# Eight pairs of heads get their mask from TensorE and their exponentials slot by slot on ScalarE; weight words travel on GpSimd's queue

## The chip, the cores and the metric

One core of one Trainium2 chip. The metric is the device time of one execution in microseconds; lower is better. Of the kernel before, three runs are known, and one further execution that was profiled.

## What is computed

Windowed attention over 8 batches and 8 heads (576 positions, 64 channels), plain windows of 32 in the first four heads and windows of 32 with a step of 4 in the other four, followed by a gated two-layer block with a convolution of three taps. Cut to what matters:

```python
scores = scale * (q @ k.T)
mask   = (rel >= 0) & (rel < 32)                  # heads 0 to 3
       | (rel >= 0) & (rel < 128) & (rel % 4 == 0)  # heads 4 to 7
scores = where(mask, scores, -1e9)
scores = scores - max(scores)
attn   = exp(scores); attn = attn / (sum(attn) + 1e-9)
x      = concat_heads(attn @ v)
h      = maximum(x @ w_in, 0)
c      = conv_w[0] * h[s-1] + conv_w[1] * h[s] + conv_w[2] * h[s+1]
out    = (h * sigmoid(c)) @ w_out
```

w_in, conv_w and w_out are given as 64-bit floats; q, k and v as 32-bit floats.

## The kernel before, in words

**Work.** A batch has four pairs of heads (`attention`, L228; pairs 0 and 1 plain, 2 and 3 with the step) and one `expert` (L352). A pair goes through these steps. *Scores* (L248): small matmuls into the PSUM buffer `att`, 18 blocks of 32 queries by 64 keys for each head, laid out as nine slots of 64 columns. *Softmax*: DVE adds the mask while it reads `att` (L254, L257), which frees `att`; it takes the maximum of each slot (L260) and subtracts it (L262); ScalarE takes the exponential of all nine slots in one instruction (L264); DVE sums (L266), adds 1e-9 (L268), takes the reciprocal (L270), multiplies (L271) and transposes into `pt` (L273). *Values* (L283): small matmuls from `pt` and `v` into `att` again. *Split*: x is kept as a high and a low part; ScalarE copies the high part out (L330), and the low part is what is left. For the first two batches (`HELPED = 2`) TensorE subtracts the high part inside `att` (`less`, L337 and L340) and ScalarE copies the rest (L343); from the third batch on DVE subtracts (L345).

There is one buffer `att` of four banks, so the scores of one pair and the values of another take turns in it; `pt` and `qk` have two buffers, `s`, `z`, `v` and `out` three.

The expert multiplies x with w_in, three matmuls of 288 columns per 128 by 128 block (high by high, high by low, low by high; L363), ScalarE applies the ReLU (L370), the convolution and the gate alternate between ScalarE and DVE (L381, L375 twice, L386, L388, L390, L392) and give the eight parts g0 to g7, and the second product takes those (L405), copied out by L412. Each product of a batch has 192 matmuls.

**Weights** (`weights`, L423). A block of 128 by 512 64-bit words is loaded into a buffer `out` (L431), and turned into a high and a low part: L438 on ScalarE, L440, L443, L445, L448, L451 on DVE. For the first ten blocks TensorE adds the pieces (L460, L461, L462) and ScalarE copies both parts (L457, L465); for the last six DVE does it (L467, L473).

**Order.** Nothing of this is in program order. `Planner.order` (L113) is a list scheduler with booked costs, latencies and due times; it runs when the kernel is built and writes each engine's instructions in the order of its plan. `DUE`, `PAIR`, `WI`, `WO`, `AHEAD` and `PERIOD` (L196 to L203) are those due times. On the chip each engine executes its own list in order, and what is late holds up what stands behind it. `SP` is one such list: loads of qk (L235) and v (L237), weight words (L431) and the outputs.

```python
last = plan.add("DVE", 0.68, due + 1.5, lambda: nc.vector.tensor_tensor(
    out=halves(flat()[:, 0:512]), in0=sc.t[:, 0:2, 0:256], in1=halves(mask_sb[:, kind, 0:512]), op=ALU.add),
```

Of the kernel before, what the change touches and what calls it, by code (L numbers as in the profile page):

```python
# [54 lines left out]
SCALE = 1.0 / D ** 0.5  # L55
# [18 lines left out]
class Planner:  # L74

    LATENCY = {"DVE": 0.05, "ACT": 0.05, "SP": 2.0, "E": 0.2, "S": 0.33, "T": 0.35, "V": 0.2}
    OVERLAP = {"DVE": 0.08, "ACT": 0.095}
# [80 lines left out]
def attn_moe(ctx: ExitStack, tc: tile.TileContext, qk_p, qk_d, v_p, v_d, w_in, w_out, conv, mask, out):  # L158
    nc = tc.nc
    const = ctx.enter_context(tc.tile_pool(name="const", bufs=1))  # L160
# [37 lines left out]
    WI, WO = (-20.4, -20.4, -7.2, -7.2, -3.1, -0.1, 7.8, 7.8), (17.2, 17.2, 36.3, 36.3, 36.9, 34.9, 43.2, 43.2)  # L198
    AHEAD = (9.1, 0.8, 0.7)
    PERIOD = 55.1  # L200
    for b in range(2, B):
        DUE[b] = tuple(t + PERIOD * b for t in (-5.1, 5.4, 33.0))
        PAIR[b] = tuple(t + PERIOD * b for t in (-21.7, -18.8, -17.2, -13.1))  # L203
    SUMMED = 10
    HELPED = 2

# [21 lines left out]
    def attention(b, p):  # L228
# [22 lines left out]
        last = plan.add("PE", (0.8, 0.92)[kind], due, scores, [lq], [qk, sc, s], "S")  # L251
        flat = lambda: s.t.rearrange("p a k -> p (a k)")
        halves = lambda t: t.rearrange("p (h k) -> p h k", h=2)
        last = plan.add("DVE", 0.68, due + 1.5, lambda: nc.vector.tensor_tensor(  # L254
            out=halves(flat()[:, 0:512]), in0=sc.t[:, 0:2, 0:256], in1=halves(mask_sb[:, kind, 0:512]), op=ALU.add),
            [last], [sc, s])
        last = plan.add("DVE", 0.215, due + 1.5, lambda: nc.vector.tensor_tensor(  # L257
            out=flat()[:, 512:576], in0=sc.t[:, 2, 0:W], in1=mask_sb[:, kind, 512:576], op=ALU.add), [last], [sc, s])
        wide = lambda t: t.unsqueeze(2).to_broadcast([128, 9, W])
        last = plan.add("DVE", 0.755, due + 2.0, lambda: nc.vector.tensor_reduce(  # L260
            out=m.t, in_=s.t, axis=AX.X, op=ALU.max), [last], [s, m])
        last = plan.add("DVE", 0.755, due + 2.5, lambda: nc.vector.tensor_tensor(  # L262
            out=s.t, in0=s.t, in1=wide(m.t), op=ALU.subtract), [last], [s, m])
        last = plan.add("ACT", 0.685, due + 3.0, lambda: nc.scalar.activation(  # L264
            out=s.t, in_=s.t, func=AF.Exp, scale=SCALE), [last], [s], "exp")
# [36 lines left out]

        last = plan.add("PE", (0.9, 0.85)[kind], due + 6.0, values, [lv, last], [v, pt, tv, x], "V")

# [23 lines left out]
        his = []  # L328
        for i, cost in ((1, (0.25, 0.3)[kind]), (0, (0.62, 1.12)[kind])):
            last = plan.add("ACT", cost, due + 7.0, lambda i=i: nc.scalar.copy(out=dst(x.t[0], i), in_=val(i)),  # L330
                            [last, *his], [tv, x])
            his.append(last)
        if b < HELPED:
            def less():
                main, rest = parts(x.t[0])
                for t in range(4):
                    nc.tensor.matmul(tv.t[:, t, 0:128], minus, main[:, t], start=False, stop=True,  # L337
                                     skip_group_check=True)
                for g in range(2):
# [83 lines left out]
    def weights(src, n, due, dst=None, pair=None, summed=False):  # L423
# [59 lines left out]
    nc.vector.tensor_copy(out=slot_masks[0][:, 0:5:4, :], in_=kinds_sb[:, 0:2, :])  # L483
    nc.vector.tensor_copy(out=slot_masks[1], in_=spread(2, 9))
    nc.vector.tensor_copy(out=slot_masks[1][:, 0:5:4, :], in_=spread(3, 2))
    nc.vector.tensor_copy(out=slot_masks[1][:, 8, :], in_=kinds_sb[:, 4, :])
    for h, in hs:
# [89 lines left out]
```

## Time and profile before

| | |
|---|---|
| median of three runs | 549.02 us (548.75 to 549.81) |
| the profiled execution | 548.65 us, of it 546.9 us span |
| PE busy | 520.8 us, 95% of the span |
| DVE busy | 410.0 us, 75% |
| ACT busy | 289.7 us, 53% |
| granted TensorE clock, mean of the span | 0.991 |

The span runs from the first to the last instruction that the profiler recorded; the profiled execution's own time is 1.75 us longer. A busy share is a mean over stages that differ, so it says little by itself: the rows further down are read by stretch.

### The profile page before, as it was taken

What the parts mean: (1) busy time and instruction counts of PE and PEld (TensorE: products, weight loads), DVE (VectorE), ACT (ScalarE), POOL (GpSimd) and SP (SyncE); (2) the same over time, 40 slices, a digit from 0 to 9 for tenths busy, and PEclk for the clock granted to TensorE, in tenths of its full rate; (3) what the DMA queues carried; (4) which work ended last, traced back from release to release, by engine and by line L of the source; (5) the groups of instructions that cost most, each with busy time, mean ns of one, the idle gap of its engine ahead of it and who ended that gap; (6) DMA issues with size and microseconds to landing.
All of it is one profiled execution on the core that took longest, in us unless ns stands there. A gap on an engine that the chain in (4) does not pass through costs nothing.

```text
span 546.9 us, 19084 instructions
## 1 busy us (share of the span) xinstructions
PE 520.8 (95%) x8664; PEld 496.5 (91%) x8664; DVE 410.0 (75%) x695; ACT 289.7 (53%) x556; POOL 0.9 (0%) x12
## 2 busy tenths in 40 slices
PE   3599978999999999999999999999999999999997
PEld 2578877999999999999999999999989999999997
DVE  5978999899996389937997399837987289936910
ACT  2466775755742586227742586227732486327721
POOL 0000000000000000000000000000000000000000
PEclk9999997999999999999999999999999999999999
DMA  7765614331135003530144103530045102300011
GB/s 251 267 196 177 207 42 155 100 121 44 50 99 162 18 23 109 163 104 23 52 146 150 30 23 96 170 111 23 28 146 168 35 23 65 112 26 23 0 44 45
DMA packets 17073, 52.32 MB, mean 96 GB/s; under 512 B 2016, under 2 KB 3168, under 8 KB 16992
## 3 DMA queue, kind: packets, MB, share of 16 engines
q1 hardware_dynamic: 16848, 51.02, 28.4%
q8 instruction: 68, 1.11, 0.9%
q10 hardware_dynamic: 144, 0.08, 0.1%
q14 instruction: 13, 0.11, 0.1%
HBM read 41.66 MB, written 9.44 MB: 93 GB/s over the span
## 4 chain that ended last, share of the span: by engine, by line
PE 88%; DVE 8%; ACT 2%; DMA 2%; issue 1%; DVEq 0%; ACTq 0%
PE nn L405 38%; PE mm L363 33%; PE att L283 8%; PE att L248 5%; DVE c L375 2%; PE nn L460 1%; DMA qk<-in_qk_d_dram 1%; PE att L337 1%; DVE s L254 1%; DVE s L262 1%; DVE c L388 1%; DVE m L260 1%; DMA qk<-in_qk_p_dram 1%; DVE pt L273 1%; DVE s L271 1%
## 5 line engine op out<-in xcount | busy, mean ns | idle before, releaser
L375 DVE SCALAR_TENSOR_TENSOR c<-h,conv_sb,c 128x576 f32<-128x576 f32 x128 | 104.0, 815 | 53.2 <-ACT c L381 51.6
L370 ACT ACTIVATE h<-mm 128x288 f32<-128x288 f32 x120 | 48.8, 408 | 49.7 <-PE mm L363 49.5
L412 ACT COPY out<-nn 128x288 f32<-128x288 f32 x64 | 25.3, 397 | 76.4 <-PE nn L405 70.9
L283 PEld LDWEIGHTS att<-pt,v 32*64 32x64 f32 x3072 | 41.4, 140 | 14.8 <-DVE s L257 4.6
L388 DVE TENSOR_TENSOR c<-c,h 128x576 f32<-128x576 f32 x64 | 47.6, 755 | 9.2 <-ACT c L386 7.7
L283 PE MATMUL att<-pt,v 32*64 32x64 f32 (+2 forms) x3072 | 44.9, 234 | 9.3 <-DVE s L257 3.5
L381 ACT ACTIVATE c<-h,conv_sb 128x576 f32<-128x576 f32 x64 | 49.6, 776 | 1.3
L248 PE MATMUL att<-qk 64*32 64x64 f32 x2432 | 36.2, 235 | 10.9 <-DMA qk<-in_qk_d_dram 5.6
L248 PEld LDWEIGHTS att<-qk 64*32 64x32 f32 x2432 | 30.1, 111 | 16.8 <-issue 5.7
L386 ACT ACTIVATE c<-c 128x576 f32<-128x576 f32 x64 | 42.5, 679 | 2.8 <-DVE c L375 2.3
L363 PE MATMUL mm<-x2a,wi 128*128 128x288 f32 x144 | 40.5, 296 | 0.0
L363 PE MATMUL mm<-x1a,wi 128*128 128x288 f32 x144 | 40.3, 296 | 0.0
L363 PE MATMUL mm<-x3a,wi 128*128 128x288 f32 x144 | 40.3, 295 | 0.0
L363 PE MATMUL mm<-x0a,wi 128*128 128x288 f32 x144 | 40.3, 295 | 0.0
L405 PE MATMUL nn<-g2a,wo 128*128 128x288 f32 x128 | 36.9, 303 | 0.0
L405 PE MATMUL nn<-g6a,wo 128*128 128x288 f32 x128 | 36.7, 300 | 0.0
L405 PE MATMUL nn<-g0a,wo 128*128 128x288 f32 x128 | 36.4, 299 | 0.2
L405 PE MATMUL nn<-g1a,wo 128*128 128x288 f32 x128 | 36.5, 300 | 0.0
L405 PE MATMUL nn<-g3a,wo 128*128 128x288 f32 x128 | 36.4, 299 | 0.0
L405 PE MATMUL nn<-g5a,wo 128*128 128x288 f32 x128 | 36.4, 299 | 0.0
L405 PE MATMUL nn<-g4a,wo 128*128 128x288 f32 x128 | 36.4, 299 | 0.0
L405 PE MATMUL nn<-g7a,wo 128*128 128x288 f32 x128 | 36.0, 300 | 0.1
(194 smaller groups left out, 1482.6 us busy)
## 6 DMA issues: line engine op xcount, KB each, us to landing
qk<-in_qk_d_dram SPq DMA_DIRECT2D x16, 664.0 KB, 4.4
qk<-in_qk_p_dram SPq DMA_DIRECT2D x16, 592.0 KB, 5.0
out_dram<-out SPq DMA_DIRECT2D x28, 288.0 KB, 2.3
v<-in_v_d_dram SPq DMA_DIRECT2D x16, 384.0 KB, 3.4
v<-in_v_p_dram SPq DMA_DIRECT2D x16, 384.0 KB, 3.5
out<-in_w_in_dram SPq DMA_DIRECT2D x8, 512.0 KB, 5.4
out<-in_w_out_dram SPq DMA_DIRECT2D x8, 512.0 KB, 4.6
out_dram<-out SPq DMA_DIRECT2D x8, 144.0 KB, 1.8
```

The costliest lines, as they stand in the source:

```text
L248: nc.tensor.matmul(sc.t[quad * 32:quad * 32 + 32, slot // 4, slot % 4 * W:slot % 4 * W + W], q, k, start=i == 0, stop=i == len(parts) - 1, ...
L254: last = plan.add("DVE", 0.68, due + 1.5, lambda: nc.vector.tensor_tensor(out=halves(flat()[:, 0:512]), in0=sc.t[:, 0:2, 0:256], in1=halve ...
L260: last = plan.add("DVE", 0.755, due + 2.0, lambda: nc.vector.tensor_reduce(out=m.t, in_=s.t, axis=AX.X, op=ALU.max), [last], [s, m])
L283: nc.tensor.matmul(tv.t[hd * 64:hd * 64 + 64, bank, o:o + n], v.t[quad * 32:quad * 32 + 32, block // 2, block % 2 * 64:block % 2 * 64 + 64 ...
L363: nc.tensor.matmul(ps.t[:, 0:HALF], wi[jw][fc][:, k * 128:k * 128 + 128], x[k].t[jx][:, hf * HALF:hf * HALF + HALF], start=(k == 0 and i = ...
L370: relu.append(plan.add("ACT", 0.4, due + 1.6 * u + 1.6, lambda fc=fc, hf=hf, ps=ps: nc.scalar.activation(out=h[fc].t[:, 1 + hf * HALF:1 + ...
L375: nc.vector.scalar_tensor_tensor(out=c[fc].t, in0=h[fc].t[:, k:S + k], scalar=conv_sb[:, k, fc:fc + 1], in1=c[fc].t, op0=ALU.mult, op1=ALU ...
L381: t = plan.add("ACT", 0.777, d, lambda fc=fc: nc.scalar.activation(out=c[fc].t, in_=h[fc].t[:, 1:S + 1], func=AF.Copy, scale=conv_sb[:, 1, ...
L386: t = plan.add("ACT", 0.686, d + 1.0, lambda fc=fc: nc.scalar.activation(out=c[fc].t, in_=c[fc].t, func=AF.Sigmoid), [t], [c[fc]], "sigmoid")
L388: t = plan.add("DVE", 0.755, d + 1.5, lambda fc=fc: nc.vector.tensor_tensor(out=c[fc].t, in0=c[fc].t, in1=h[fc].t[:, 1:S + 1], op=ALU.mult ...
L405: nc.tensor.matmul(ps.t[:, 0:HALF], wo[jw][2 * dm + k // 4][:, k % 4 * 128:k % 4 * 128 + 128], g[k].t[jg][:, hf * HALF:hf * HALF + HALF], ...
L412: outs.append(plan.add("ACT", 0.4, out_due + 3.3 + 3.3 * u, lambda hf=hf, ps=ps, o=o: nc.scalar.copy(out=o.t[:, hf * HALF:hf * HALF + HALF ...
```

## The change

The first eight pairs (`EASED = 8`: batches 0 and 1) take another way through the softmax. TensorE puts the mask into `att` first (three matmuls of an identity `ones` with the bf16 mask, 256, 256 and 64 columns), and the scores are added to it. DVE takes the maximum straight from `att` and scales it by the negative factor. ScalarE takes the exponential slot by slot, nine instructions that read `att`, each with one column of the maximum as bias and one column of `z` as the place of its sum. `HELPED = 0` takes `less` away: DVE subtracts the high part in all batches. Weight words are loaded by GpSimd's queue instead of SP's. The masks themselves are built by ScalarE instead of DVE. The due times and some booked costs of the planner are new, so that the order on all engines is new as well.

```diff
-    DUE = {0: (-9.2, 2.8, 30.4), 1: (64.7, 50.1, 92.3)}
-    PAIR = {0: (-26.0, -24.7, -23.0, -27.0), 1: (-4.9, 1.3, 8.9, 14.5)}
+    DUE = {0: (-4.7, 3.9, 23.7), 1: (69.8, 44.0, 102.5)}
+    PAIR = {0: (-42.0, -47.4, -47.0, -39.2), 1: (-4.4, -28.5, -16.5, -8.4)}
...
-    HELPED = 2
+    EASED = 8
+    HELPED = 0
...
+            if eased:
+                for bank, (c0, c1) in enumerate(((0, 256), (256, 512), (512, 576))):
+                    nc.tensor.matmul(sc.t[:, bank, 0:c1 - c0], ones, mask_sb[:, kind, c0:c1], start=True, stop=True,
+                                     skip_group_check=True)
...
-                                         start=i == 0, stop=i == len(parts) - 1, skip_group_check=True)
+                                         start=i == 0 and not eased, stop=i == len(parts) - 1, skip_group_check=True)
...
+        if eased:
+            last = plan.add("DVE", 0.68, due + 1.5, lambda: nc.vector.tensor_reduce(
+                out=m.t[:, 0:8].rearrange("p (h a) -> p h a", h=2),
+                in_=sc.t[:, 0:2, 0:256].rearrange("p h (a k) -> p h a k", k=W), axis=AX.X, op=ALU.max), [last], [sc, m])
+            last = plan.add("DVE", 0.215, due + 1.5, lambda: nc.vector.tensor_reduce(
+                out=m.t[:, 8:9], in_=sc.t[:, 2, 0:W], axis=AX.X, op=ALU.max), [last], [sc, m])
+            last = plan.add("DVE", 0.173, due + 2.0, lambda: nc.vector.tensor_scalar(
+                out=m.t, in0=m.t, scalar1=-SCALE, scalar2=None, op0=ALU.mult), [last], [m])
+            def exps():
+                for i in range(9):
+                    nc.scalar.activation(out=s.t[:, i, :], in_=sc.t[:, i // 4, i % 4 * W:i % 4 * W + W], func=AF.Exp,
+                                         scale=SCALE, bias=m.t[:, i:i + 1], accum_out=z.t[:, i:i + 1])
+            last = plan.add("ACT", 2.2, due + 3.0, exps, [last], [sc, s, m, z], "exp")
...
-        last = plan.add("SP", 1.75 * f, due - AHEAD[2], lambda: nc.sync.dma_start(
+        last = plan.add("POOL", 2.2 * f, due - AHEAD[2], lambda: nc.gpsimd.dma_start(
...
+    nc.scalar.copy(out=ones, in_=ident)
-    nc.vector.tensor_copy(out=slot_masks[0], in_=spread(2, 9))
+    nc.scalar.copy(out=slot_masks[0], in_=spread(2, 9))
```

The last line stands for five copies of this kind. Three places of the new order:

**ACT, start of the program, before** (`minus` is the negative identity, `wi` a weight part, `w0a` and `w1a` scratch of two weight blocks, `s` a pair's softmax):

```order
L475 DMA kinds_sb<-in_mask_dram 128x320
L477 ACT_TABLE_LOAD
L477 ACTIVATE minus<-ident 128x128
L264 ACTIVATE s_103<-s_103 128x576
L264 ACTIVATE s_104<-s_104 128x576
L264 ACTIVATE s_105<-s_105 128x576
L438 ACTIVATE w0a<-out_150 128x512
L438 ACTIVATE w1a<-out_151 128x512
L330 CAST x0a<-att_159 128x64
```

and now:

```order
L499 DMA kinds_sb<-in_mask_dram 128x320
L507 ACT_TABLE_LOAD
L507 COPY mask_sb<-kinds_sb 128x576
L509 COPY mask_sb<-kinds_sb 128x576
L508 COPY mask_sb<-kinds_sb 128x2x64
L510 COPY mask_sb<-kinds_sb 128x2x64
L511 COPY mask_sb<-kinds_sb 128x64
L462 ACTIVATE w0a<-out_151 128x512
L501 ACTIVATE minus<-ident 128x128
L502 CAST ones<-ident 128x128
L274 ACTIVATE s_104,z_110<-att_160,m_107 128x64 x9
L481 CAST wi_67<-w0b 128x512
```

The five mask copies and the first weight block's L462, which waits for the weight words, now stand ahead of `ones`, and `ones` ahead of everything that TensorE does.

**PE, start of the program, before** (L248 scores, L283 values, L337 and L340 `less`):

```order
L248 MATMUL att_159<-qk_98 32x64 x40
L248 MATMUL att_159<-qk_99 32x64 x36
L248 MATMUL att_159<-qk_98 32x64 x36
L248 MATMUL att_159<-qk_99 32x64 x40
L283 MATMUL att_159<-pt_112,v_100 64x64 x24
L283 MATMUL att_159<-pt_112,v_100 64x32 x8
L283 MATMUL att_159<-pt_112,v_100 64x16 x16
L337 MATMUL att_159<-x0a,minus 128x128 x4
L340 MATMUL att_159<-x0a,minus 128x32 x2
L283 MATMUL att_159<-pt_113,v_101 64x32 x8
```

and now, the second pair's end and what follows (L255 scores, L484 to L486 the sum of the first weight block):

```order
L248 MATMUL att_160<-mask_sb,ones 128x256
L248 LDWEIGHTS ones
L248 MATMUL att_160<-mask_sb,ones 128x64
L255 MATMUL att_160<-qk_100 32x64 x40
L484 MATMUL nn_163<-w0b,ident 128x512
L485 MATMUL nn_163<-r_158,minus 128x512
L486 MATMUL nn_163<-wi_67,minus 128x512
L248 LDWEIGHTS ones
L248 MATMUL att_160<-mask_sb,ones 128x256
```

Mask matmuls stand ahead of each pair's scores, the first weight sum stands between the second and the third pair, and no `less` is left.

**DVE, the first pair, before:**

```order
L254 TENSOR_TENSOR s_103<-att_159,mask_sb 128x512
L257 TENSOR_TENSOR s_103<-att_159,mask_sb 128x64
L260 TENSOR_REDUCE m_106<-s_103 128x9
L262 TENSOR_TENSOR s_103<-s_103,m_106 128x576
L254 TENSOR_TENSOR s_104<-att_159,mask_sb 128x512
L257 TENSOR_TENSOR s_104<-att_159,mask_sb 128x64
L260 TENSOR_REDUCE m_107<-s_104 128x9
L266 TENSOR_REDUCE z_109<-s_103 128x9
L262 TENSOR_TENSOR s_104<-s_104,m_107 128x576
```

and now (L464 to L475 are a weight block's five steps):

```order
L264 TENSOR_REDUCE m_107<-att_160 128x8
L267 TENSOR_REDUCE m_107<-att_160 128x1
L269 TENSOR_SCALAR m_107<-m_107 128x9
L464 TENSOR_SCALAR w0a<-w0a 128x512
L467 TENSOR_SCALAR w0b<-w0a 128x512
L469 SCALAR_TENSOR_TENSOR w0b<-out_151,w0b 128x512
L472 TENSOR_SCALAR w0a<-w0b 128x512
L475 SCALAR_TENSOR_TENSOR r_158<-out_151,w0a 128x512
L292 TENSOR_SCALAR z_110<-z_110 128x9
L294 RECIPROCAL z_110<-z_110 128x9
L295 TENSOR_TENSOR s_104<-s_104,z_110 128x576
L297 STREAM_TRANSPOSE pt_113<-s_104 128x576
L264 TENSOR_REDUCE m_108<-att_160 128x8
```

The pair keeps seven DVE instructions of ten, and a whole weight block stands between its maximum and its reciprocal.

## Rows read from the trace of the kernel before

**Rows 1.** The page, busy tenths of TensorE and its granted clock, 40 slices of 13.7 us.
```profile
PE   3599978999999999999999999999999999999997
...
PEclk9999997999999999999999999999999999999999
```

**Rows 2.** Busy time by stretch: length, PE, weight loads, DVE, ACT, POOL, granted clock, DMA.
```profile
0.00:96.04 96.04, 75.15 (x1672) 64.22 (x1673) 83.02 (x162) 55.01 (x109) 0.91 (x12) 0.95 0.56 185
96.04:516.00 419.96, 418.95 (x6800) 406.52 (x6801) 321.10 (x527) 227.66 (x433) 0.00 (x0) 1.00 0.25 79
516.00:546.90 30.90, 26.71 (x195) 25.74 (x194) 5.91 (x8) 7.00 (x14) 0.00 (x0) 1.00 0.12 40
...
82.00:90.00 8.00, 6.53 (x109) 5.16 (x109) 7.83 (x15) 3.19 (x9) 0.00 (x0) 0.50 0.39 121
```

**Rows 3.** Timeline, first 8 us: start, duration, engine, line, operation.
```profile
0.73 0.40 ACTq L475 DMA_DIRECT2D kinds_sb<-in_mask_dram  x1
...
5.71 0.45 DVE L482 COPY mask_sb<-kinds_sb 128x576 bf16<-128x576 bf16 x1 [5.71 <-DMA kinds_sb<-in_mask_dram]
...
7.20 0.69 DVE L254 TENSOR_TENSOR s<-att,mask_sb 128x512 f32<-128x512 f32 x1 [0.36 <-PE att L248]
```

**Rows 4.** Timeline of DVE: one pair, 45.88 to 51.85 us; L345 from the groups.
```profile
45.88 0.68 DVE L254 TENSOR_TENSOR s<-att,mask_sb 128x512 f32<-128x512 f32 x1
...
48.19 0.81 DVE L375 SCALAR_TENSOR_TENSOR c<-h,conv_sb,c 128x576 f32<-128x576 f32 x1
...
49.82 0.17 DVE L268 TENSOR_SCALAR z<-z 128x9 f32<-128x9 f32 x1
...
51.07 0.78 DVE L273 STREAM_TRANSPOSE pt<-s 128x576 f32<-128x576 f32 x1
...
L345 DVE TENSOR_TENSOR x0b<-att,x0a 128x512 fp32r<-128x512 f32 x4 | 2.7, 681 | 4.3 <-ACT x0a L330 4.3
```

**Rows 5.** Timeline of DVE: first and last of the five instructions on one weight block.
```profile
39.45 0.43 DVE L440 TENSOR_SCALAR w0a<-w0a 128x512 f32<-128x512 f32 x1 [1.11 <-ACT w0a L438]
...
41.63 0.69 DVE L451 SCALAR_TENSOR_TENSOR r<-out,w0a 128x512 fp32r<-128x512 uint32 x1
```

**Rows 6.** Groups of ACT by shape: shapes, count, busy us, mean ns, idle before.
```profile
L381 ACT ACTIVATE c<-h,conv_sb 128x576 f32<-128x576 f32 x64 | 49.6, 776 | 1.3
...
L264 ACT ACTIVATE s<-s 128x576 f32<-128x576 f32 x32 | 21.3, 684 | 22.5 <-DVE s L262 22.4
...
L390 ACT CAST g1a<-c 128x576 fp32r<-128x576 f32 x8 | 5.4, 676 | 1.0 <-DVE c L388 1.0
...
L330 ACT CAST x0a<-att 128x512 fp32r<-128x512 f32 x5 | 3.0, 593 | 0.0
...
L330 ACT CAST x0a<-att 128x64 fp32r<-128x64 f32 x5 | 1.1, 213 | 9.8 <-PE att L283 8.0 <-DVE s L271 1.9
```

**Rows 7.** The chain that ended last, 70 to 97 us: start, duration, piece.
```profile
81.92 0.71 ACT x5a L330 x2
...
82.68 1.11 PE att L337 x4
83.79 0.36 PE att L340 x2
...
84.92 2.05 PE att L283 x79
86.98 2.00 PE nn L460 x2
...
92.36 1.29 PE att L283 x81
...
95.44 0.47 PE att L337 x4
```

**Rows 8.** SP's queue, 0 to 110 us: line, releaser, us, times, longest.
```profile
SPq L237 <- PE att L283: 47.4, 7, 14.4
...
SPq L431 <- DVE r L451: 10.7, 5, 3.4
```

More of the change, by code (lines that the diff above doesn't have):

```diff
@@ L74 @@
 class Planner:
-    LATENCY = {"DVE": 0.05, "ACT": 0.05, "SP": 2.0, "E": 0.2, "S": 0.33, "T": 0.35, "V": 0.2}
+    LATENCY = {"DVE": 0.05, "ACT": 0.05, "SP": 2.0, "POOL": 3.0, "E": 0.2, "S": 0.33, "T": 0.35, "V": 0.2}
     OVERLAP = {"DVE": 0.08, "ACT": 0.095}
@@ L166, in attn_moe @@
     ident = const.tile([128, 128], F32, name="ident")
+    ones = const.tile([128, 128], BF16, name="ones")
     minus = const.tile([128, 128], F32R, name="minus")
@@ L248, in scores @@
                         nc.tensor.matmul(sc.t[quad * 32:quad * 32 + 32, slot // 4, slot % 4 * W:slot % 4 * W + W], q, k,
-                                         start=i == 0, stop=i == len(parts) - 1, skip_group_check=True)
-        last = plan.add("PE", (0.8, 0.92)[kind], due, scores, [lq], [qk, sc, s], "S")
+                                         start=i == 0 and not eased, stop=i == len(parts) - 1, skip_group_check=True)
+        last = plan.add("PE", (0.8, 0.92)[kind] + (0.5 if eased else 0.0), due, scores, [lq], [qk, sc, s], "S")
@@ L252, in attention @@
         flat = lambda: s.t.rearrange("p a k -> p (a k)")
         halves = lambda t: t.rearrange("p (h k) -> p h k", h=2)
[L254 to L258, printed above, removed]
@@ L259, in attention @@
-        wide = lambda t: t.unsqueeze(2).to_broadcast([128, 9, W])
[L260 to L265, printed above, removed]
@@ L266, in attention @@
-        last = plan.add("DVE", 0.755, due + 3.5, lambda: nc.vector.tensor_reduce(
-            out=z.t, in_=s.t, axis=AX.X, op=ALU.add), [last], [s, z])
+        wide = lambda t: t.unsqueeze(2).to_broadcast([128, 9, W])
+        if eased:
[11 more added lines that the diff above has]
+            last = plan.add("ACT", 2.2, due + 3.0, exps, [last], [sc, s, m, z], "exp")
+        else:
+            last = plan.add("DVE", 0.68, due + 1.5, lambda: nc.vector.tensor_tensor(
+                out=halves(flat()[:, 0:512]), in0=sc.t[:, 0:2, 0:256], in1=halves(mask_sb[:, kind, 0:512]), op=ALU.add),
+                [last], [sc, s])
+            last = plan.add("DVE", 0.215, due + 1.5, lambda: nc.vector.tensor_tensor(
+                out=flat()[:, 512:576], in0=sc.t[:, 2, 0:W], in1=mask_sb[:, kind, 512:576], op=ALU.add), [last], [sc, s])
+            last = plan.add("DVE", 0.755, due + 2.0, lambda: nc.vector.tensor_reduce(
+                out=m.t, in_=s.t, axis=AX.X, op=ALU.max), [last], [s, m])
+            last = plan.add("DVE", 0.755, due + 2.5, lambda: nc.vector.tensor_tensor(
+                out=s.t, in0=s.t, in1=wide(m.t), op=ALU.subtract), [last], [s, m])
+            last = plan.add("ACT", 0.685, due + 3.0, lambda: nc.scalar.activation(
+                out=s.t, in_=s.t, func=AF.Exp, scale=SCALE), [last], [s], "exp")
+            last = plan.add("DVE", 0.755, due + 3.5, lambda: nc.vector.tensor_reduce(
+                out=z.t, in_=s.t, axis=AX.X, op=ALU.add), [last], [s, z])
@@ L301, in values @@
                             pv(2 * hd + g, hd, g, 8 + 2 * kh + r, c0 + 16 * r, 128 + 16 * r, 16)
-        last = plan.add("PE", (0.9, 0.85)[kind], due + 6.0, values, [lv, last], [v, pt, tv, x], "V")
+        last = plan.add("PE", (1.1, 1.25)[kind], due + 6.0, values, [lv, last], [v, pt, tv, x], "V")
         def parts(t):
@@ L328, in attention @@
         his = []
-        for i, cost in ((1, (0.25, 0.3)[kind]), (0, (0.62, 1.12)[kind])):
+        for i, cost in ((1, 0.21), (0, 0.6)):
             last = plan.add("ACT", cost, due + 7.0, lambda i=i: nc.scalar.copy(out=dst(x.t[0], i), in_=val(i)),
@@ L343, in attention @@
             return [plan.add("ACT", cost, due + 7.5, lambda i=i: nc.scalar.copy(out=dst(x.t[1], i), in_=val(i)),
-                             [last], [tv, x]) for i, cost in ((0, (0.62, 1.12)[kind]), (1, (0.25, 0.3)[kind]))]
+                             [last], [tv, x]) for i, cost in ((0, 0.6), (1, 0.21))]
         return [plan.add("DVE", cost, due + 7.5, lambda i=i: nc.vector.tensor_tensor(
             out=dst(x.t[1], i), in0=val(i), in1=dst(x.t[0].bitcast(F32), i), op=ALU.subtract), his, [tv, x])
-            for i, cost in ((0, (0.68, 1.0)[kind]), (1, (0.215, 0.25)[kind]))]
+            for i, cost in ((0, 0.69), (1, 0.215))]
     TERMS = ((0, 0), (0, 1), (1, 0))
@@ L477, in attn_moe @@
     nc.scalar.mul(out=minus, in_=ident, mul=-1.0)
+    nc.scalar.copy(out=ones, in_=ident)
     spread = lambda i, n: kinds_sb[:, i, :].unsqueeze(1).to_broadcast([128, n, W])
     slot_masks = [mask_sb[:, kind, :].rearrange("p (a k) -> p a k", k=W) for kind in range(2)]
-    nc.vector.tensor_copy(out=slot_masks[0], in_=spread(2, 9))
[L483 to L486, printed above, removed]
+    nc.scalar.copy(out=slot_masks[0], in_=spread(2, 9))
+    nc.scalar.copy(out=slot_masks[0][:, 0:5:4, :], in_=kinds_sb[:, 0:2, :])
+    nc.scalar.copy(out=slot_masks[1], in_=spread(2, 9))
+    nc.scalar.copy(out=slot_masks[1][:, 0:5:4, :], in_=spread(3, 2))
+    nc.scalar.copy(out=slot_masks[1][:, 8, :], in_=kinds_sb[:, 4, :])
     for h, in hs:
```

11 lines of the change are left out of this document (6 added, 5 removed).

## Prediction

> **What bounds the kernel now.** I read the page's slices first, then the stretches, then the start and the chain. The page shows TensorE near full from the third slice on, with a dip in the sixth and seventh; in the seventh its clock falls too [rows 1]. By stretch [rows 2]: from 96.04 to 516 us PE idles about 1 us in 420, so that part lasts as long as its matmuls. The end (516 to 546.9) idles 4.2 us behind the last convolution and output. The rest, 20.89 us (96.04 - 75.15), lies before 96.04, where DVE is busy for 83.02 us, 86%. So the start is bound by DVE, which prepares weights and softmaxes, and everything after it by TensorE. In 82 to 90 us the clock is granted at 0.50, the lower of its two levels (1.2 GHz) [rows 2], behind the stretch in which PE waited for DVE.
>
> The two orders end alike, and behind the start the matmuls are the same. So I compare one point: when the second product of batch 0 begins and PE has run out of waits. In the order before, all scores, values, `less`, ten weight sums and batch 0's first product are done by 96.04, and 15 matmuls of the second (2.1 us). The new order reaches that point, without those 15, at its first L429. What that point's time gains or loses, the end gains or loses.
>
> **PE's work up to there.** Removed: eight `less`. One takes 1.47 us at half clock (1.11 + 0.36) and 0.47 and a short tail, 0.6 to 0.7, at full [rows 7]; two at the first price and six at 0.66 make 6.9 us. Added: eight masks of 576 columns. No row shows them; the nearest is the same `less`, 576 columns in six matmuls, which bounds one from above at 0.6 and 1.47 us; half of 0.6, for three loads in place of six, is the lower end. I take 0.7 for the three early ones and 0.35 for five: +3.9 (ends 2.4 and 7.4). Work at half clock: in 82 to 90 us PE is busy 6.53 us [rows 2], 2.0 of it `less`; the rest (values 2.05 against 1.29 later [rows 7], a weight sum) would take half, -2.3, and a value step at 80 us and the fourth scores, which now come later, -1.0. The new order has no wait there long enough, by my walk, for the clock to fall as it did. Sum: -6.9 + 3.9 - 3.3 = -6.3 us.
>
> **One pair on DVE and ACT.** Before, the ten DVE instructions from 45.88 to 51.85 take 5.2 us without the tap of 0.81 that stands among them [rows 4]. Now: maximum 1.05 (0.68, 0.21 and a small one of 0.17), then from L268's place to the transpose's end 2.0 (49.82 to 51.85), and the low part of x, 0.9 (0.681 [rows 4] and its tail): 3.95. So 1.2 us less per pair, but the maximum cannot start before the mask is in `att`.
>
> ACT's nine exponentials, E per pair, decide most. A copy of 128x64 from PSUM takes 0.213 us, and two copies, 0.213 + 0.593, take 0.71 together: 0.10 overlaps [rows 6, 7]. So a bare slot costs 0.11. A column as operand costs 0.10: L381, with one, 0.776, L390, without, 0.676 [rows 6]: 0.21. What the sum into `z` costs, no row shows: nothing at best, at worst an instruction of its own per slot, 0.11 to 0.21 more. Bounds of E: 9 x 0.11 = 1.1, and 9 x 0.42 = 3.8. I take 0.255 a slot, E = 2.3 with the last one's tail: the row with an operand, and under half of an extra instruction. Before, it was one of 0.684.
>
> **The waits, walked along the new order.** `att` is the chain: it is held through scores, maximum and all nine exponentials, where before the mask add freed it.
> - Start. The mask kinds land at 5.71 [rows 3]. Five mask copies on ACT (two of 576 columns like L390's 0.676, three small like L330's 0.213, each overlapping by 0.10 [rows 6]) end near 7.6; the first weight block's L462, 0.67 for its 512 columns, `minus` and `ones` at 0.3 each follow: TensorE starts at 8.75. DVE's first softmax step, at 7.20 before [rows 3], moves to 10.8; its own mask copies, of which L482 is the first, are gone and hid nothing.
> - The first three pairs: masks and scores 2.0 to 2.3, maximum 1.05, E 2.3, while DVE does a weight block (39.45 to 42.32, 2.9 [rows 5]) and the previous pair's 2.0. PE waits 3.5, 1.65 and 1.85 us for `att`; a weight sum fills the gaps. Then three value steps, each followed by the copies 0.71 and the low part 0.9: 1.75 and 1.65, and 0.15 before the fourth scores. Their end: 38.05. Waits so far 19.3. From there the first product flows.
> - From 38.05 to the second product: eight more waits, 0.3 to 1.2 us each, before value steps, scores and two weight sums: 5.0. DVE has some 48 us of work there (five softmax ends 10.0, four maxima 4.2, five weight blocks 14.5, four low parts 3.6, eleven taps of 0.81, ten gate steps of 0.67), ACT some 45 (five E are 11.5 of it), in 53 us. None has much room, but no single wait is long.
>
> Waits 24.3 against 20.89: +3.4. Behind the point, g5 comes 1.0 us late, since five tables and copies stand ahead of it on ACT; before, nothing waited there: +1.0.
>
> **The weight words.** On SP they waited for buffers with others behind: 10.7 us for weight scratch, and v's loads 47.4 for `att` users [rows 8]. The new SP order has no weights and POOL nothing else after its start, so neither queue holds the other. In my walk each block has 5 us or more between its buffer and its use, so I put the move at nothing; cover: the ACT and DVE work ahead of each L462. The first block is the exception, without cover: it stands ahead of `ones`, and each us that it lands after 7.5 moves everything.
>
> The Trainium skill (SBUF — State Buffer, SBUF: two separate sides) says that a DVE instruction in a two-port mode locks GpSimd out, so that descriptors of transfers issued there are written only after it. That speaks against this move. Weighed against the trace: a 128x512 tensor_scalar takes 0.43 us where two-operand steps of that size take 0.69 [rows 5], so the weight steps may be such instructions; by the rule a transfer would start up to 0.43 us later for each it meets, which the 5 us cover.
>
> **Sum.** 548.65 - 6.3 + 3.4 + 1.0 = 546.75 for the profiled execution; the median is 0.37 above it: **547.1 us**. Walked with E = 2.05 the point comes 1.5 us earlier, with 2.8 some 3 later: 6 us for each us of E.
>
> **Rivals.**
> - *Dear slots* (slower). The sum into `z` is an instruction of its own that adds 0.1 or more to a slot. At 0.31, E = 2.8, the time is 550.1; at 0.42, E = 3.8, 556. It decides from 0.29 a slot (E = 2.6), where the change is worth nothing. For it: `att` is the chain and E its largest link; nothing hides it in the first 38 us. Against: no row has a second instruction. Chance 0.33.
> - *Late first words* (no change or slower). GpSimd's queue or the shared transfers bring the first block at 9.5 to 11.5 instead of 7.5: +2 to +4, 549 to 551. For: four large loads of SP are asked for in the same microseconds. Against: it is issued among the first. Later blocks late by the lock above would end here too. Chance 0.13.
> - *Cheap slots, covered waits* (faster). At 0.21 a slot or less, with two or three of the small waits filled: 541.5 to 545. For: DVE has 1.2 us less per pair. Against: ACT has more than before. Chance 0.13.
> - That the change doesn't do what it says is out: the order shows mask matmuls, nine exponentials and weight loads on POOL.
>
> **Numbers.** Forecast 0.41 (545 to 549.5). A measurement here tells 0.2%, 1.1 us. Faster: three quarters of the forecast, all of the cheap case, a little of the others: 0.46. Same: 0.21. Slower: most of the dear slots, half of the late words: 0.33. Range: the mask's bounds (-1.5, +3.5) and E from 1.8 to 3.5 give 542.5 to 554.5.
>
> **What would show it.** Right: ACT's L274 at 0.25 to 0.27 from start to start; first scores near 9.5 us; PE idle of about 24 us before its first L429 near 91, and no half clock after 38. Wrong: a second ACT instruction per slot, POOL transfers that take over 6 us, DVE idle between 40 and 90, or new PE waits behind 100 us for w_out's last blocks.

## Result: 0.5% slower

The changed kernel takes 551.86 us (median of 7 runs, 550.80 to 553.48), the kernel before beside it 549.41 (7 runs): ratio 1.0051, 95% interval 1.0032 to 1.0069. The forecast was 547.1, faster; the time lies inside the range given, on the other side of no change.

The profiled execution took 552.48 us, span 550.7. The page of the changed kernel, TensorE's slices and its clock, to be held against [rows 1]:

```profile
PE   1578999999999999999999999999999999999997
...
PEclk9968999999999999999999999999999999999999
```

TensorE starts later (its first matmul at 9.91 us, 5.56 in the kernel before), then fills up without the dip of before. By stretch (columns as in [rows 2]; the first ends at the point of the prediction, the first L429):

```profile
0.00:95.16 95.16, 69.84 (x1633) 56.11 (x1633) 70.36 (x148) 66.52 (x235) 8.41 (x26) 0.93 0.54 184
95.16:130.00 34.84, 34.84 (x260) 34.53 (x261) 33.87 (x57) 20.58 (x40) 1.70 (x3) 1.00 0.21 74
130.00:516.00 386.00, 382.58 (x6526) 370.51 (x6526) 288.92 (x474) 203.61 (x390) 0.00 (x0) 1.00 0.25 80
```

The point is at 95.16, where about 91 was forecast. With the 2.1 us of products that the order before had already done, 97.26 stands against 96.04: +1.2. Behind it the new order needs 453.4 us (550.7 - 97.26), the old one 450.9 (546.9 - 96.04): +2.6. Together +3.8 between the two profiled spans; the medians differ by 2.45. DVE works 12.7 us less in the start than before, as meant, but the start isn't shorter. The waits of TensorE there say why (who waits, on whom; us in total, times, longest):

```profile
PE att L248 <- ACT ones L502: 9.9, 1, 9.9
PE att L307 <- ACT s L274: 5.8, 4, 3.0
PE att L248 <- ACT s L274: 5.6, 3, 4.0
PE att L307 <- DVE x0b L369: 1.6, 1, 1.6
PE att L307 <- DVE x1b L369: 1.6, 1, 1.6
```

9.9 us pass before the first matmul, and TensorE waits 11.4 us for the nine exponentials. ACT's groups by shape (count, busy us, mean ns) show of what a slot consists, and the timeline how two follow each other:

```profile
L274 ACT ACTIVATE s<-att,m 128x64 f32<-128x64 f32 x72 | 21.4, 327 | 12.0 <-DVE m L269 10.0 <-DVE w0a L464 2.0
L274 ACT ACTIVATION_READ_ACCUMULATOR s<-att,m 128x1 f32 x72 | 15.8, 220 | 0.0
```
```profile
13.32 0.30 ACT L274 ACTIVATE s<-att,m 128x64 f32<-128x64 f32 x1
13.51 0.20 ACT L274 ACTIVATION_READ_ACCUMULATOR s<-att,m 128x1 f32 x1
13.61 0.31 ACT L274 ACTIVATE s<-att,m 128x64 f32<-128x64 f32 x1
```

Each slot has a second instruction, the read of the sum: 0.29 us from slot to slot, 2.78 us for nine (13.01 to 15.78). The start on ACT and TensorE:

```profile
6.64 0.24 ACT L511 COPY mask_sb<-kinds_sb 128x64 bf16<-128x64 bf16 x1
8.82 0.66 ACT L462 ACTIVATE w0a<-out 128x512 f32<-128x512 f32 x1 [1.94 <-DMA out<-in_w_in_dram]
9.38 0.29 ACT L501 ACTIVATE minus<-ident 128x128 fp32r<-128x128 f32 x1
9.58 0.28 ACT L502 CAST ones<-ident 128x128 bf16<-128x128 f32 x1
9.91 0.66 PE L248 MATMUL att<-mask_sb,ones 128*128 128x256 bf16 x3 [9.91 <-ACT ones L502]
```

The masks are ready at 6.9. ACT then waits 1.94 us for the first weight words, issued at 1.43 on GpSimd's queue, and `ones`, which needs nothing of them, stands behind that wait. Behind the point, TensorE's groups between 130 and 516 us (busy, mean ns, idle before), first of the changed kernel, then of the kernel before:

```profile
L307 PE MATMUL att<-pt,v 32*64 32x64 f32 (+2 forms) x2304 | 32.8, 225 | 3.3 <-issue 3.2
```
```profile
L283 PE MATMUL att<-pt,v 32*64 32x64 f32 (+2 forms) x2304 | 31.8, 225 | 0.0
L248 PE MATMUL att<-qk 64*32 64x64 f32 x1752 | 24.7, 224 | 0.9 <-issue 0.9
```

The values lose 3.2 us in five gaps for which the profile names no wait. So there are three suspects: dear slots; `ones` behind the first words, perhaps because of the queue; and the new order itself, in the start or behind it.

### The profile page after: what moved, and what is told of

Its sections match the earlier page's. It is cut to its first block, busy times and chain, and to the rows that moved or that the text cites. A ratio compares the mean times of both kernels' runs of the same rounds, so it can differ in the third digit from the quotient of the medians.

```text
span 550.7 us, 19152 instructions
## 1 busy us (share of the span) xinstructions
PE 518.0 (94%) x8640; PEld 490.9 (89%) x8640; DVE 402.9 (73%) x690; ACT 301.0 (55%) x682; POOL 10.1 (2%) x29
## 4 chain that ended last, share of the span: by engine, by line
PE 83%; ACT 9%; DVE 4%; DMA 1%; issue 1%; POOL 0%; ACTq 0%; DVEq 0%; POOLq 0%
PE nn L429 38%; PE mm L387 32%; PE att L307 7%; PE att L255 5%; ACT s L274 4%; DMA out<-in_w_in_dram 1%; ACT h L394 1%; DVE m L264 1%; PE nn L484 1%; DVE pt L297 1%; ACT c L405 1%; DVE c L399 1%; DVE s L295 1%; ACT c L410 0%; ACT w1a L462 0%
## 5 line engine op out<-in xcount | busy, mean ns | idle before, releaser
L405 ACT ACTIVATE c<-h,conv_sb 128x576 f32<-128x576 f32 x64 | 49.5, 777 | 0.9
L429 PE MATMUL nn<-g2a,wo 128*128 128x288 f32 x128 | 37.0, 304 | 0.0
L429 PE MATMUL nn<-g0a,wo 128*128 128x288 f32 x128 | 36.6, 301 | 0.2
L429 PE MATMUL nn<-g5a,wo 128*128 128x288 f32 x128 | 36.7, 303 | 0.0
L429 PE MATMUL nn<-g3a,wo 128*128 128x288 f32 x128 | 36.6, 300 | 0.0
L429 PE MATMUL nn<-g1a,wo 128*128 128x288 f32 x128 | 36.3, 299 | 0.0
L429 PE MATMUL nn<-g6a,wo 128*128 128x288 f32 x128 | 36.3, 300 | 0.0
L387 PE MATMUL mm<-x4a,wi 128*128 128x288 f32 x128 | 35.8, 295 | 0.0
L387 PE MATMUL mm<-x6a,wi 128*128 128x288 f32 x128 | 35.8, 294 | 0.0
L429 PE MATMUL nn<-g4a,wo 128*128 128x288 f32 x128 | 35.8, 294 | 0.0
L387 PE MATMUL mm<-x5a,wi 128*128 128x288 f32 x128 | 35.8, 295 | 0.0
```

The source lines that it names most:

```text
L387: nc.tensor.matmul(ps.t[:, 0:HALF], wi[jw][fc][:, k * 128:k * 128 + 128], x[k].t[jx][:, hf * HALF:hf * HALF + HALF], start=(k == 0 and i = ...
L405: t = plan.add("ACT", 0.777, d, lambda fc=fc: nc.scalar.activation(out=c[fc].t, in_=h[fc].t[:, 1:S + 1], func=AF.Copy, scale=conv_sb[:, 1, ...
L429: nc.tensor.matmul(ps.t[:, 0:HALF], wo[jw][2 * dm + k // 4][:, k % 4 * 128:k % 4 * 128 + 128], g[k].t[jg][:, hf * HALF:hf * HALF + HALF], ...
```

## Experiments

The ratios are taken over all runs; they differ from the quotients of the medians by up to 0.002. The last column is the start of the second product of batch 0 in the profiled execution.

| kernel | us, median | us of before beside it | ratio (95%) | first L429 at |
|---|---|---|---|---|
| changed | 551.86 | 549.41 | 1.0051 (1.0032 to 1.0069) | 95.16 |
| no sums | 546.75 | 549.12 | 0.9969 (0.9949 to 0.9990) | 90.0 |
| `ones` by DVE | 548.38 | 549.12 | 0.9986 (0.9972 to 0.9999) | 92.0 |
| words by SP | 549.40 | 549.12 | 1.0005 (0.9990 to 1.0019) | 92.1 |
| `ones` by DVE, words by SP | 548.26 | 548.15 | 0.9999 (0.9982 to 1.0016) | 91.2 |
| before, words by GpSimd | 551.76 | 549.12 | 1.0053 (1.0034 to 1.0072) | 94.3 (L405; 91.8 before) |
| two exponentials | 553.13 | 548.15 | 1.0080 (1.0055 to 1.0105) | 95.9 |
| the same, `ones` by DVE | 548.48 | 548.15 | 1.0012 (0.9993 to 1.0030) | 91.4 |
| order alone | 582.79 | 548.15 | 1.0627 (1.0600 to 1.0653) | 107.2 |
| old steady due times | 553.88 | 549.51 | 1.0090 (1.0069 to 1.0111) | 91.9 |
| the same, no maximum | 559.57 | 549.51 | 1.0182 (1.0150 to 1.0214) | 91.4 |
| no maximum, two exponentials | 542.45 | 548.95 | 0.9876 (0.9862 to 0.9890) | 85.6 |
| no maximum, sums kept | 540.70 | 548.95 | 0.9869 (0.9840 to 0.9898) | 83.5 |
| spaced values, no maximum | 537.24 | 549.26 | 0.9782 (0.9762 to 0.9802) | 84.4 |
| spaced values, `ones` by DVE | 544.76 | 549.26 | 0.9929 (0.9907 to 0.9951) | 91.1 |

**The dear slots.**

```diff
-scale=SCALE, bias=m.t[:, i:i + 1], accum_out=z.t[:, i:i + 1])
+scale=SCALE, bias=m.t[:, i:i + 1])
```

This kernel leaves the sums out; `z` holds ones from the start.

> The changed kernel, the order of every engine kept, without the sums of the exponentials: the sum of each slot is left out, and z holds ones from the start. If the second instruction of each slot (the read of the accumulated sum, 220 ns, 72 of them) is what makes the slots dear, a slot takes 0.19 to 0.22 us from start to start instead of 0.29, nine take 1.8 to 2.0 us instead of 2.78, and by 6 us for each us of E the second product of batch 0 begins near 90 us instead of 95.16: 546.5 to 548 us, 4 to 5.5 us under the changed kernel and under the kernel before. If the new order and due times cost the time, or the late start of TensorE, it stays within 1 us of 551.9.

```profile
13.46 1.96 ACT L276 ACTIVATE s<-att,m 128x64 f32<-128x64 f32 x9 [3.15 <-DVE m L271]
```

Nine exponentials take 1.96 us, 0.82 less, and the point comes 5.2 us earlier, though the first scores start 0.45 later (10.36): 5.6 to 0.82, or 6.9 us for each us of E. The prediction had 6. So the dear slots are shown, with their price: the read costs the changed kernel some 4.5 us (the ratios differ by 0.0082, 0.8% of 549).

**The late `ones`.** Only the engine that makes `ones` changes:

```diff
-    nc.scalar.copy(out=ones, in_=ident)
+    nc.vector.tensor_copy(out=ones, in_=ident)
```

> The changed kernel with ones made by VectorE, which is idle until 11.9 us, so that the first scores don't wait behind ScalarE's pass over the first weight block. Theory of the late first words: the first scores begin near 7.0 instead of 9.91, and if that start moves everything behind it, 549 us (2.9 us less). Theory of the dear slots: ScalarE and the one score buffer run the start, and the first pair being early is taken back in part by the next waits: 550 to 551.5 us. If the weight blocks on VectorE and not the pairs set the start, no change, 551.9.

```profile
2.55 0.23 DVE L502 CAST ones<-ident 128x128 bf16<-128x128 f32 x1 [2.55 <-POOL ident masks.py:199]
6.59 0.64 PE L248 MATMUL att<-mask_sb,ones 128*128 128x256 bf16 x3 [6.59 <-ACT mask_sb L508]
9.09 0.66 ACT L462 ACTIVATE w0a<-out 128x512 f32<-128x512 f32 x1 [2.20 <-DMA out<-in_w_in_dram]
```

The start moves by 3.3 us and the point by 3.2, nearly one to one, though the words land no earlier. That removes the loss: level with the kernel before, if not a little under it. That later waits would take part of it back, as the theory of the dear slots had it, was wrong.

**The queue.** In both kernels only the engine that issues the weight words changes, not the order:

```diff
-last = plan.add("POOL", 2.2 * f, due - AHEAD[2], lambda: nc.gpsimd.dma_start(
+last = plan.add("POOL", 2.2 * f, due - AHEAD[2], lambda: nc.sync.dma_start(
```

> The changed kernel with the order of all work kept, the weight words issued by SyncE again instead of GpSimd. If the queue is worth nothing (the prediction put it at nothing), 551.9 within 0.6 us. If the words come later behind the loads of q, k and v in SyncE's queue, or these loads wait behind a weight load that waits for its buffer (up to 41 us in GpSimd's queue now), it is slower: 553 us or more. If GpSimd's own issuing is what delays the first words (7.4 us from issue to landing), 549 to 551.

> The kernel before with its order kept and only the weight words issued by GpSimd. If the queue is worth nothing, 549.4 within 0.6 us. If GpSimd's issuing is dear (2 to 3 us more to land the first block, from which VectorE's start depends), 550.5 to 552; if SyncE's queue held loads up behind buffers, 547 to 548.5.

In the changed kernel SyncE issues the first words at 0.74, ahead of all else on its queue, and they are there when ACT comes to them:

```profile
6.48 0.65 ACT L462 ACTIVATE w0a<-out 128x512 f32<-128x512 f32 x1
7.24 0.28 ACT L502 CAST ones<-ident 128x128 bf16<-128x128 f32 x1
7.58 0.34 PEld L248 LDWEIGHTS <-ones 128*128 128x128 bf16 x3 [7.58 <-ACT ones L502]
```

It gains 2.5 us by the ratios, where `ones` by DVE gained 3.6, and the point comes to the same place (92.1 and 92.0). The kernel before, given GpSimd's queue, loses 2.6 us, but elsewhere. The first scores of TensorE there, and the third of the kernel before:

```profile
5.22 1.60 PE L248 MATMUL att<-qk 64*32 64x64 f32 x80 [5.22 <-DMA qk<-in_qk_d_dram]
7.74 1.34 PE L248 MATMUL att<-qk 64*32 64x64 f32 x72 [0.92 <-DVE s L257]
14.41 1.33 PE L248 MATMUL att<-qk 64*32 64x64 f32 x72 [5.33 <-DMA qk<-in_qk_p_dram]
```
```profile
10.96 1.30 PE L248 MATMUL att<-qk 64*32 64x64 f32 x70 [1.54 <-DMA qk<-in_qk_p_dram]
```

Before, SyncE's queue issued the words at 11.55, behind the loads of q and k, and the third scores waited 1.5 us. On a queue of their own the words go out at 1.44 and 2.43, and the third q and k, issued at 6.85, share the transfers with them (407 GB/s from 8 to 14 us, 289 before): the wait is 5.3, and the first L405 comes 2.5 us later. So a queue of its own also takes away an order among loads.

> The changed kernel with ones made by VectorE and the weight words issued by SyncE. If both edits gave their 2.5 to 3.5 us by the same thing, the first scores no longer waiting for the first words by way of ones, it is where each alone is: 548 to 549.5. If they are two costs, 545.5 to 546.5.

Both edits together give what `ones` by DVE gives alone (0.9999 and 0.9986, the intervals overlap). It was one cost: `ones` behind the first words. With that gone, the queue of the words is worth nothing that these runs can tell.

**Shorter exponentials, the sum on DVE.** Two exponentials stand for nine, with one maximum a partition for the first 512 columns and one for the last 64.

```diff
...
-for i in range(9):
-    nc.scalar.activation(out=s.t[:, i, :], in_=sc.t[:, i // 4, i % 4 * W:i % 4 * W + W], func=AF.Exp,
-                         scale=SCALE, bias=m.t[:, i:i + 1], accum_out=z.t[:, i:i + 1])
+nc.scalar.activation(out=halves(flat()[:, 0:512]), in_=sc.t[:, 0:2, 0:256], func=AF.Exp,
+                     scale=SCALE, bias=m.t[:, 0:1])
+nc.scalar.activation(out=s.t[:, 8, :], in_=sc.t[:, 2, 0:W], func=AF.Exp, scale=SCALE, bias=m.t[:, 1:2])
...
+nc.vector.tensor_reduce(out=z.t, in_=s.t, axis=AX.X, op=ALU.add)
```

> The changed kernel with its order kept; ScalarE makes the exponentials of an eased pair in two instructions (512 columns of banks 0 and 1, 64 of bank 2) with one maximum per partition for each, without the summing reads, and VectorE sums them (one more instruction of 0.755 us a pair, behind the hold of the score buffer). Dear slots: E falls from 2.78 to about 0.95 us (0.68 and 0.25), 1.8 us a pair; the waits on these exponentials are 11.4 us in the changed kernel, of which the sum on VectorE gives some back, so 5 to 9 us less: 543 to 547. If E is not what the start waits for beyond what e1 showed, 546 to 548. If new order and due times cost the time: 551.9 within 1.

> As the run with two exponentials, and ones made by VectorE. If the late start and the dear slots are two costs in one row of work, they add up: 3 to 3.5 us less than the run with two exponentials. If the weight blocks on VectorE (or the weight words) set the start once the pairs are quick, it gives under 1.5 us.

The first missed by 6 us or more; the second takes 4.6 us less than the first, so here too the late start counts in full. E falls to 0.9 us, and the point doesn't move (95.9 and 91.4, against 95.16 and 92.0). Groups of ACT and DVE of the first of the two:

```profile
L272 ACT ACTIVATE s<-att,m 128x512 f32<-128x512 f32 x8 | 5.5, 687 | 15.7 <-DVE m L268 11.6 <-DVE w0a L468 4.1
L274 ACT ACTIVATE s<-att,m 128x64 f32<-128x64 f32 x8 | 2.5, 308 | 0.0
```
```profile
L294 DVE TENSOR_REDUCE z<-s 128x9 f32<-128x576 f32 x8 | 6.0, 747 | 0.0
```

DVE works 6.0 us more, eight sums, in a row of work with few gaps (18.9 of the 20 us from 12 to 32, 16.7 in the changed kernel); ACT now waits for DVE's maximum 11.6 us instead of 10.0. TensorE's work before the point grows as well, from 69.8 to 71.4 us, at a granted clock of 0.89 instead of 0.93. So E doesn't price the start alone: VectorE's row stands next to it. The read of the sum cost ACT 0.8 us a pair, the sum costs DVE 0.75.

**The order alone, and old due times for the steady part.**

```diff
-    EASED = 8
+    EASED = 0
...
-    nc.scalar.copy(out=ones, in_=ident)
```

> The changed kernel with no pair eased: masks added by VectorE for all pairs, one exponential, as in the kernel before; the new due times, costs, the queue of the weight words and the subtraction on VectorE stay, ones is not made. If the new order itself costs the time, about 552 or more, and the eased pairs are worth little. If the eased pairs are the loss (2.78 us on the score buffer against 3.2 us of VectorE's chain) it is faster than the changed kernel: 548 to 551. By the prediction's walk the eased pairs save VectorE some 2.8 us a pair, so without them 555 or more.

582.8: with these due times, pairs whose masks and sums are DVE's cost over 30 us more. The two belong together, so this run prices neither the order nor the eased pairs alone. For the gaps behind the point, `ones` by DVE with the due times of before from batch 2 on:

```diff
-    PERIOD = 57.2
+    PERIOD = 55.1
...
-        DUE[b] = tuple(t + PERIOD * b for t in (-5.3, 11.1, 32.3))
-        PAIR[b] = tuple(t + PERIOD * b for t in (-21.1, -18.7, -17.6, -13.5))
+        DUE[b] = tuple(t + PERIOD * b for t in (-5.1, 5.4, 33.0))
+        PAIR[b] = tuple(t + PERIOD * b for t in (-21.7, -18.8, -17.2, -13.1))
```

> The changed kernel with ones made by VectorE (548.4 us in its own run) and, from the third batch on, the period and due times of the kernel before. If the gaps of TensorE without a named wait between 130 and 516 us (2.2 to 4.8 us in all kernels with the new due times, 0.5 to 0.9 with the old) come from the new steady order, in which a values group follows the scores after 9 products and the next values after 12, they fall to under 1.5 us and the time by 1 to 2 us: 546.4 to 547.4. If they belong to something else that the change brings, 548.4 within 0.6 and gaps of 2 us or more.

The gaps are gone (0.2 us between 130 and 516), as expected, but not the time: real waits came in their place, of scores for DVE above all. Over the span TensorE idles 3.1 us more than with `ones` by DVE alone and works 2.0 us more (granted clock 0.981 and 0.988), and the time is 5.5 us longer:

```profile
PE att L255 <- DVE s L282: 2.4, 2, 1.4
PE nn L429 <- ACT g6a L414: 0.5, 1, 0.5
```

**Without the maximum.** A first try, on the old steady due times and planned anew, prices nothing: its `ones` fell behind two steps of a weight block on DVE, and TensorE began at 10.6. At 559.6 us it missed both of its forecasts, and its point comes no earlier.

> As the run with the old steady due times, but an eased pair's exponentials are made without a maximum, straight from the score buffer in two instructions, and VectorE sums them: the maximum is left out (the scores of these inputs are small). The score buffer is then held 0.95 us instead of 3.8 us, and VectorE works 0.3 us less a pair; costs in the plan accordingly, so the start has a new order. If the hold of the one score buffer sets the start: 4 us or more less than the run with the old steady due times, 542 to 543.5. If by now VectorE's row of work (the weight blocks and the pairs) sets it, 0 to 2 us less: 544.5 to 547.

The other two keep the changed kernel's order of TensorE, and make `ones` on DVE first:

```diff
-            last = plan.add("DVE", 0.68, due + 1.5, lambda: nc.vector.tensor_reduce(
...
-                out=m.t, in0=m.t, scalar1=-SCALE, scalar2=None, op0=ALU.mult), [last], [m])
+for cost, at in ((0.68, 1.5), (0.215, 1.5), (0.173, 2.0)):
+    last = plan.add("DVE", cost, due + at, lambda: None, [last], [sc, m])
...
```

> The changed kernel, TensorE's order kept, ones made by VectorE at the start, and in eased pairs no maximum (it is left out; the scores of these inputs are small): two exponentials straight from the score buffer, summed by VectorE. The buffer is held about 0.95 us instead of 3.85, VectorE works 0.3 us less a pair. If the hold of the score buffer sets the start, at least 4 us under the run with ones by VectorE (548.4): 544 or less. If VectorE's row of work took over, as with two exponentials and a shared maximum, 546.5 to 548.5.

> As the run above with the nine exponentials and their summing reads on ScalarE kept: only the maximum is left out. The buffer is held 2.8 us instead of 3.85, VectorE works 1.07 us less a pair, ScalarE the same. If the hold sets the start (6 us for each us of it): 6 us under 548.4, 542 to 543.5. If VectorE's row sets it: 1 to 4 us less, 544.5 to 547.5, and below the run with two exponentials. If ScalarE's first wait (for the first weight words, 9.1 us, ahead of the first exponentials on its queue) sets it: 548 within 0.6.

They are 6 and 7.7 us under `ones` by DVE; the second is below its forecast for the hold of `att`, 542 to 543.5. In the second the nine took 1.9 us, not the 2.8 of its expectation: without the column operand a slot is shorter too. Its groups on ACT, and the stretches:

```profile
L269 ACT ACTIVATE s<-att 128x64 f32<-128x64 f32 x72 | 14.8, 244 | 2.0 <-PE att L255 1.5 <-ACT w1a L457 0.5
L269 ACT ACTIVATION_READ_ACCUMULATOR s<-att 128x1 f32 x72 | 14.6, 230 | 0.0
```
```profile
0.00:83.50 83.50, 66.69 (x1633) 54.83 (x1633) 63.28 (x125) 60.11 (x234) 8.52 (x26) 0.94 0.62 209
83.50:516.00 432.50, 429.43 (x6870) 416.57 (x6871) 332.45 (x543) 231.96 (x442) 1.69 (x3) 1.00 0.24 78
```

The kernel that holds `att` 1.9 us reaches the point 2.1 us before the one that holds it 0.9, though in time the two can't be told apart (0.9869 and 0.9876). DVE works 63.3 us up to the point in the one and 68.4 in the other (0 to 85.6). This fits a start that is a chain through both engines, with the maximum in it on each: three instructions on DVE, a column operand on ACT.

**Spacing the values.** In the changed kernel's steady part, 9 products stand between the last scores and the next values, 12 between these and the next, 15 before the last; in the kernel before, whose values lose nothing, 15 or more stand at each of these places. Of the changed kernel's five gaps three lie inside the values that follow on the 12 products, and one each in the group ahead of these and the one behind. Timeline of TensorE in the changed kernel:

```profile
232.31 1.26 PE L307 MATMUL att<-pt,v 32*64 32x32 f32 x96
233.50 0.40 PE L429 MATMUL nn<-g5a,wo 128*128 128x288 f32 x1
...
235.07 0.29 PE L429 MATMUL nn<-g0a,wo 128*128 128x288 f32 x1
235.30 0.89 PE L307 MATMUL att<-pt,v 32*64 32x64 f32 x64
236.77 0.65 PE L307 MATMUL att<-pt,v 32*64 32x16 f32 x32 [0.59 <-issue]
```

The edit draws products that are ready ahead of such a values group until 15 stand between the groups (in the loop that runs the plan; `space` counts steps of three products since the last scores or values):

```diff
+if t.table == "V" and t.due > 90:
+    for j in range(i + 1, i + 60):
+        p = tasks[j] if j < len(tasks) else None
+        if space >= 5 or p is None:
+            break
...
+        p.run()
+        run.add(p)
+        space += 1
```

> The run without the maximum (540.7), with two to three products each moved ahead of the first and second values group of batches 2 to 7, so that 15 products instead of 9 and 12 stand between the scores, the values and the next values; everything before 95 us as it was. If the gaps of TensorE without a named wait (2.3 us in five of them there, all in the values group after 9 and 12 products) come from groups of short matmuls standing too close, they fall under 0.8 us in all and the time to 538.5 to 539.5. If they hang on something else, 540.7 within 0.8 and gaps of 2 us or more, or they move to another group.

> The run with ones made by VectorE (548.4, gaps of 2.4 us) with the same spacing of the values groups. Close groups: gaps under 0.8 us and 546 to 547. Something else: 548.4 within 0.8, gaps of 2 us or more.

The medians of both fall by some 3.5 us, more than the gaps. The values in 130 to 516 us, with `ones` by DVE, and then with the spacing:

```profile
L307 PE MATMUL att<-pt,v 32*64 32x64 f32 (+2 forms) x2304 | 32.8, 225 | 2.3 <-issue 2.2
```
```profile
L307 PE MATMUL att<-pt,v 32*64 32x64 f32 (+2 forms) x2304 | 31.6, 225 | 0.0
```

The 2.2 us of gaps are gone, and the groups are busy 1.2 us less: a group with a gap in it counts 0.89 and 0.65, a whole one 1.36, so each gap costs some 0.2 us more than it lists. All waits of TensorE between 130 and 516 us are now 0.6 us. So the spacing of the groups of short matmuls is the cause behind the point.

What TensorE lacks in these pauses can be found in the trace. The page of the changed kernel lists a queue that loads instructions:

```profile
q8 instruction: 67, 1.10, 0.8%
```

That is one packet of 16 KB for some 256 of TensorE's 17,340 instructions. Counted through the trace, all five pauses stand at the same place in a row of 256 instructions, and each ends 1.3 to 1.5 us after such a packet has ended. In all sixteen traces the pauses without a named wait between 130 and 516 us stand at that place, but for two of 0.2 us. So TensorE has run out of instructions: a values group is 192 of them in 1.3 us, 15 products are 30 in 2.2 us. This is read from where the pauses fall; no run changes the loading itself.

The spaced kernel with the maximum kept, 0.9929, beats both kernels; without the maximum it is 0.9782, but there the guard against large scores is given up.

## Why the prediction was wrong

Its sum was 548.65 - 6.3 + 3.4 + 1.0 = 546.75 for the profiled execution; 552.48 was measured, 5.7 more. By its own steps:

- **ACT's nine exponentials, E = 2.3: the step that failed.** The sum was taken at 0.045 us a slot, "under half of an extra instruction"; it is an instruction of its own. A slot takes 0.29 us, 0.20 without the read and 0.20 without the operand; if the parts add up, a bare slot, the operand and the read cost about 0.1 us each. Bare slot (0.11) and operand (0.10) were read rightly from [rows 6]; the read was the mis-sized term, 0.09 instead of 0.045. E was 2.78 (nine times 0.255 had no room for the last slot's tail either); at 6 us for each us that is +2.9. The rival *dear slots* is what happened, 550.1 by its own price.
- **First words at 7.5.** They landed at 8.8, and TensorE began at 9.91 instead of 8.75: +1.15. The rival *late first words* is this, and the passage on the words gave the mechanism, "each us that it lands after 7.5 moves everything"; the two runs that took `ones` from behind the words show it. Its chance was held down by "it is issued among the first". That was true (1.43) and not enough: 7.4 us to land, as in the kernel before (6.4 to 8.9 for its first three). Issued first on SyncE's queue, the block took 3.9.
- **The point.** 2.9 + 1.15 is 4.05: the walk's 93.1 (91 and the 2.1 us) becomes 97.2, and 97.26 was measured. That they agree so closely is in part luck, for the split is another: by these two terms the waits should be 28.35, and they were 25.3 (24.3 forecast), while TensorE's work fell by 3.2 instead of 6.3. Half clock came back, which the walk had not counted, in 30 to 38 us (granted 0.50) and near 52, against "no half clock after 38" (values at 2.06 at 31.04, a weight sum at 2.08 at 52.39). Masks cost 0.66 early, as taken, and 0.35 later.
- **Behind the point, +1.0 for g5.** That wait didn't come: in 95.16 to 130 TensorE never idles. +2.6 came from elsewhere, the values groups set too close, for which TensorE's instructions came too late. No step looked at the spacing of short matmuls: "behind the start the matmuls are the same". 1.6 us of the miss.
- **6 us for each us of E** held for the read (6.9) and not for E in general: where the sum moves to DVE, nothing is gained. The walk's "none has much room" was the better sentence.
- **The queue at nothing** was right for all blocks but the first, whose exception it named. On the kernel before the same move costs 2.6 us by crowding the third q and k: a cost that the sum didn't look for, since it took the new order's loads as given.
- **The lock of GpSimd** by DVE (the Trainium skill, SBUF — State Buffer, SBUF: two separate sides) was put at nothing. With the order kept, the words of w_in take 4.8 us to land on GpSimd's queue and 3.7 on SyncE's in the changed kernel, 5.5 and 5.4 in the kernel before; those of w_out 3.8 and 3.6, 4.7 and 4.6. That is 1.1 us at most, within the cover of 5; whether the lock has a part in it, no run shows.
- **Slips without weight.** The range's upper end doesn't follow from its terms: 547.1 + 3.5 + 6 x 1.2 is 557.8, not 554.5. The pair of before has nine DVE instructions, not ten; its 5.2 us are right.

## What to carry to other kernels

When an instruction gets one more output (a sum beside the result), price it as an instruction until a row shows otherwise, and multiply by how often it stands on a chain. A constant that costs 0.3 us belongs on a queue where nothing that waits for a load stands ahead of it. When a new order is costed, look at how close groups of many short matmuls come to stand, and count their instructions, not only who waits for whom; and when a load leaves a shared queue, ask which loads it used to let go first.

## What the runs showed of the hardware

- Groups of 96 short matmuls (64 by 32 and smaller) with 12 products of 0.13 us between them, 9 before the first, lost up to 2.0 us in one of the groups, mostly the second, with no wait named; with 15 between all of them, nothing over 0.2 us in these groups. The pauses stand at one place in every 256 instructions of TensorE, and end 1.1 to 1.6 us after a 16 KB packet of the instruction queue.
- Such a gap can cost twice. With `ones` by DVE and words by SP, one of 1.97 us was followed by products at the lower of the two clock levels (the granted clock of 236 to 240 us is 0.70, and products start 0.24 us apart instead of 0.13):

```profile
231.28 0.89 PE L307 MATMUL att<-pt,v 32*64 32x64 f32 x64
234.13 0.65 PE L307 MATMUL att<-pt,v 32*64 32x16 f32 x32 [1.97 <-issue]
...
236.60 0.45 PE L429 MATMUL nn<-g3a,wo 128*128 128x288 f32 x1
```

- An ACT slot of 128x64 from PSUM takes 0.20 us from start to start with either the column operand or the read of the sum, 0.29 with both.
- Moving early 512 KB loads to a second queue made a load on the first one later: TensorE's wait for the third q and k grew from 1.5 to 5.3 us.
